# Spectral mixing and a gated feed-forward on one core: the opening's first step by channel halves, the first and last spectrum units in channel parts, three weight blocks converted later

## The chip, the core and the metric

The kernel is one program on one core of a Trainium2 chip. The core has five engines with queues of their own that run side by side: TensorE (PE; its weight loads are shown as PEld), VectorE (DVE), ScalarE (ACT), GpSimd (POOL) and SyncE (SP), which here only issues transfers. Tiles lie in SBUF, matmul results in PSUM (eight banks of 512 float32 values in each of 128 partitions). The metric is the device time of one execution in microseconds, lower is better; it is shown as the median of several runs.

## The reference

Eight elements `x[b]` of 3136 positions by 256 channels are filtered in frequency along the positions, and every position then goes through a feed-forward block with a SoLU gate and a layer norm:

```python
X = np.fft.rfft(x, axis=1)
y = np.fft.irfft(X * (filt_r + 1j * filt_i)[None], n=3136, axis=1)
h = y.reshape(25088, 256) @ w_in                     # 256 -> 1024
e = np.exp(h - h.max(-1, keepdims=True))
solu = h * e / (e.sum(-1, keepdims=True) + 1e-09)
ln = (solu - mean(solu)) / np.sqrt(var(solu) + 1e-06) * g_ln
out = ln @ w_out                                      # 1024 -> 256
```

`w_in` and `w_out` come as float64 and are turned into float32 on the chip.

## The kernel before

All arithmetic is float32. The Fourier transform of 3136 = 49 x 64 positions is done as matmuls with tables in two steps each way. For most elements the data between the steps goes through DRAM. Element 0 stays in SBUF, so that the feed-forward can start early; the part of the program that does this is the opening, and it is all that the change touches.

The opening, in its order:

- **Loads.** SP issues them in order: eight pieces of x (two transfers of 192 KB each), raw weight block 0 behind piece 2 and block 2 behind piece 5 (512 KB each, `begin`, L533), then inverse tables and filters in three groups (L490, L497), weight blocks 1 and 3, small tables, and rows of element 1 (`fetch_second`, L485) into a part of the token array `y` that is not in use yet. At most eight of SP's transfers are under way: an issue waits until the transfer eight places ahead has landed.
- **First step** (L600, L605). Piece i holds 4 of 32 row groups in `rows_x`; two matmuls of 512 columns, each run as two passes, fill the two banks of one PSUM tile, which ScalarE copies back to the same place in SBUF, now named `pairs_x`, in a turned order. The last piece is copied by ScalarE and VectorE, half each. `ps_h` has three such tiles.
- **Filler.** `idle_row` (L614) gives TensorE products that nobody reads; between them `tables_back` (L510, L512) turns the tables for the way back.
- **Transposes** (`turn_rows`, L623): four VectorE transposes of 64 channels each, in place.
- **Spectrum units** (L326 to L365). Seven units, in the order 0, 1, 2, 6, 3, 4, 5. Each has a forward product on TensorE into a two-bank tile (real and imaginary part), four multiplications by the filter on VectorE (L347, L348), two additions on GpSimd (L349; for the last unit the second one on VectorE), an inverse product into two one-bank tiles of `ps_t` (two buffers), and two copies back to `pairs_x` (L365; for the last unit one on VectorE). Two units' forward products run ahead.
- **Way out.** Four more transposes; first step of element 1 (`second.first`, L251, L253), six products and copies with stores to DRAM from GpSimd's queue; then the back products (L419, L423), which fill `y` with tokens.
- **Weights.** `load_float64` (L454 to L464) turns one block of raw words into float32: one step on ScalarE, five on VectorE, two on GpSimd. Blocks 0 and 2 are converted during the first step, 1 and 3 around the last unit. The buffer `power` has two places. Four weight sums (L170) follow, since the feed-forward multiplies 2 x 2 blocks with seven products.

After that the main loop runs, one step per 128 tokens: hidden products (L799), gate and norm on VectorE, ScalarE and GpSimd, projections (L935), with the other elements' transforms put in between at fixed steps (`PLAN`). Instructions of one of these two parts keep their written order on each engine; the main loop's first ones may stand between the opening's last.

Of the kernel before, what the change touches and what calls it, by code (L numbers as in the profile page):

```python
# [9 lines left out]
FP32 = mybir.dt.float32  # L10
# [98 lines left out]
def kernel(  # L109
# [99 lines left out]
    class Spectrum:  # L209
# [114 lines left out]
        def product(self, i, out, lhsT, rhs):  # L324
            for v in range(self.units[i][1]):
                nc.tensor.matmul(out=out[:, v, :], lhsT=lhsT(v), rhs=rhs[:, v, :],  # L326
                                 start=True, stop=True)

        def forward(self, i, pss):
            t2, de = self.t2s.pop(i), self.des[i]  # L330
            for u in range(self.shape(i)[0]):
                for r in range(2):
                    block = slice(NQ * r, NQ * r + NQ)
                    self.product(i, pss[r][NQ * u:NQ * u + NQ], lambda v: de[block, v, 0, u, :],
                                 t2[block, u::2, :] if len(t2.shape) == 3 else t2[block, :, :, u])
            self.spectra[i] = pss

# [16 lines left out]
        def inverse(self, i, pss, out=None, two=False):  # L354
# [9 lines left out]
            for u in range(self.shape(i)[0]):  # L364
                (nc.vector.tensor_copy if two and u else nc.scalar.copy)(  # L365
                    out=self.gs[i][:, u:2 * w:2, :] if out is None else out[:, 0:w, :, u],
                    in_=pss[u][:, 0:w, :])
# [70 lines left out]
    with ExitStack() as st:  # L438
# [8 lines left out]
        def load_float64(dst, raw, power):  # L447
# [4 lines left out]
            ts, stt, tt = (nc.vector.tensor_scalar, nc.vector.scalar_tensor_tensor, nc.gpsimd.tensor_tensor)  # L452
# [109 lines left out]
        for i in range(pieces):  # L562
            for h in range(2):
                fetch_x(h, NCH * i, NCH, nc.sync.dma_start)
            if i in (2, 5):
                begin((0, 2)[i // 3], nc.sync.dma_start)
# [5 lines left out]
        begin(1, nc.sync.dma_start)  # L572
        begin(3, nc.sync.dma_start)
        nc.sync.dma_start(out=wf_t, in_=wf_dram)
        nc.sync.dma_start(out=wi_t, in_=wi_dram)
        nc.sync.dma_start(out=g_sb, in_=moe_g_ln.rearrange("(k p) -> p k", p=P))
        fetch_second(range(EARLY))
# [11 lines left out]

        def conversion(j):  # L590
            power = wpool.tile([P, 512], I32, name="power", tag="power", bufs=2)
            return load_float64(weights[j][0], raws.pop(j), power)

        for j in range(WARM):
            nc.tensor.matmul(out=ps_t.tile([P, P], FP32, name=f"warm_{j}", tag="t"), lhsT=blank, rhs=blank,
                             start=True, stop=True)
        for i in range(pieces):
            ps = ps_h.tile([P, 2, 512], FP32, name=f"pa_0_{i}", tag="h")
            for j in range(2):
                nc.tensor.matmul(out=ps[:, j], lhsT=wf0_t,  # L600
                                 rhs=rows_x[0:NR, NCH * i + 2 * j:NCH * i + 2 * j + 2, :],
                                 start=True, stop=True)
            size = 2 if i < pieces - 1 else 1
            for j in range(0, 2, size):
                (nc.scalar.copy, nc.vector.tensor_copy)[j](  # L605
                    out=pairs_x[:, 2 * i + j:2 * i + j + size].rearrange("p a c t -> p a t c"),
                               in_=ps[:, j:j + size].rearrange("p a (t c) -> p a t c", t=2))
            if i in (3, 6):
                for op in conversion((0, 2)[i // 4]):
                    op()  # L610

        def idle(out):

            nc.tensor.matmul(out=out, lhsT=one, rhs=one, start=True, stop=True)  # L614

        def idle_row(count, name):
            for j in range(count):
                idle(ps_h.tile([P, P], FP32, name=f"{name}_{j}", tag="h"))

        def turn_rows():  # L620
            for first in range(0, C, 64):
                part = pairs_x[:, :, first:first + 64].rearrange("p a c t -> p c a t")
                nc.vector.transpose(out=part, in_=part)  # L623

        for i0, n in ((0, 4), (4, 4)):
            idle_row(12, f"idle_{i0}")
            tables_back(i0, n)
        turn_rows()

        def start(i):  # L630
            i0, n = sp.units[i]
            sp.t2s[i] = pairs_x[:, i0:i0 + n]
            sp.fetch_filter(i)
            sp.fetch_de(i)
            sp.forward(i, halves(f"pb_0_{i}"))

# [3 lines left out]
        for i in order[:2]:  # L640
            start(i)
        tables_back(8, NP - 8)
        early_weights = [op for ops in zip(conversion(1), conversion(3)) for op in ops]
        for at, i in enumerate(order):
            if at + 2 < units:
                start(order[at + 2])
            ended = at == units - 1
            sp.multiply(i, 0, nc.gpsimd.tensor_tensor)
            sp.multiply(i, 1, (nc.vector if ended else nc.gpsimd).tensor_tensor)
            if ended:  # L650
                for op in early_weights[:6]:
                    op()
            pss = [ps_t.tile([P, 2, C], FP32, name=f"pc_0_{i}_{u}", tag="t") for u in range(2)]
            i0, n = sp.units[i]
            sp.inverse(i, pss, pairs_x[:, i0:i0 + n], ended)
        turn_rows()
# [8 lines left out]
        for op in early_weights[6:]:  # L665
            op()
# [567 lines left out]
```

## Time and profile before

| what | us |
|---|---|
| median of the three runs shown | 1574.35 |
| the three runs | 1574.35, 1943.49, 1570.65 |
| profiled execution: its own time | 1569.28 |
| profiled execution: span of the trace | 1567.5 |
| TensorE busy in the span | 1532.5 |
| VectorE, GpSimd, ScalarE busy | 1254.9, 1157.2, 927.9 |

In timeline rows the first number is the start in us from the span's start, the second the duration of the row (of all its instructions where it has a count), then engine, line, operation, tiles, shape and count; the bracket gives the engine's idle time before the row and what ended it. In the table by stretch each engine has its busy time and its number of instructions; the last three columns are TensorE's granted clock, the DMA engines' share and GB/s. A float32 matmul shows as two passes.

### The profile page before, as it was taken

The numbers are of one execution on the slowest core, as the hardware profiler recorded it, in microseconds if no ns is written. First come the engines' busy times: TensorE is split into PE (matmuls) and PEld (weight loads), VectorE is DVE, ScalarE is ACT, GpSimd is POOL, SyncE is SP. The second block draws the span as 40 slices with busy tenths as digits, with TensorE's granted clock in tenths as the row PEclk, the third lists the DMA queues.
The fourth block names the chain that finished last, engine by engine and source line by source line (L and its number), as shares of the span: only waits on it lengthen the run. The fifth ranks groups of instructions, "written<-read, shape, count | busy, mean of one in ns | idle before, by whom it ended". The sixth has DMA issues, their size and how long they took to land.

```text
span 1567.5 us, 36719 instructions
## 1 busy us (share of the span) xinstructions
PE 1532.5 (98%) x12844; PEld 1061.7 (68%) x12844; DVE 1254.9 (80%) x2233; ACT 927.9 (59%) x1898; POOL 1157.2 (74%) x1346
## 2 busy tenths in 40 slices
PE   8988999999999999999999999999999999999997
PEld 5633576667666776667766776667776777777777
DVE  4879878897998789878998698877998777776773
ACT  3565655666556656666566655666556666666663
POOL 2578886697879678887779767786766767676665
PEclk9999999999999999999999999999999999999999
DMA  9768788877987689667886588766874545343434
GB/s 246 252 202 226 218 225 220 227 212 207 252 242 204 173 236 254 196 173 192 249 230 190 152 229 247 203 184 176 233 204 119 138 122 135 88 115 102 116 104 118
DMA packets 342256, 298.07 MB, mean 190 GB/s; under 512 B 27915, under 2 KB 311573, under 8 KB 342073
## 3 DMA queue, kind: packets, MB, share of 16 engines
q1 hardware_dynamic: 278872, 175.82, 42.5%
q0 software_dynamic: 29568, 87.33, 18.6%
q10 hardware_dynamic: 33634, 32.58, 7.2%
q8 instruction: 104, 1.70, 0.5%
q14 instruction: 78, 0.64, 0.1%
HBM read 118.02 MB, written 74.84 MB: 123 GB/s over the span
## 4 chain that ended last, share of the span: by engine, by line
PE 59%; DMA 2%; DVE 0%; SPq 0%; issue 0%; POOL 0%; ACT 0%; ACTq 0%; POOLq 0%
PE o L935 26%; PE m L799 26%; PE py L396 2%; PE pc L326 1%; PE pa L294 1%; PE pb L326 1%; DMA solu_t<-turn 1%; DMA x<-in_x_dram 0%; SPq L880 0%; DMA out_dram<-ot 0%; PE o L899 0%; POOL u L778 0%; ACT e L833 0%; DVE h L845 0%; DVE h L820 0%
## 5 line engine op out<-in xcount | busy, mean ns | idle before, releaser
L935 PEld LDWEIGHTS o<-w_out_sb,solu_t 128*128 128x128 f32 x3136 | 381.1, 192 | 47.3 <-issue 43.5
L799 PE MATMUL m<-w_in_sb,s 128*128 128x512 f32 x784 | 398.4, 609 | 5.8 <-ACT h L809 3.3
L935 PE MATMUL o<-w_out_sb,solu_t 128*128 128x128 f32 x3136 | 400.2, 276 | 1.7 <-DVE ot L955 1.6
L935 PEld LDWEIGHTS o<-w_out_sb,u 128*128 128x128 f32 x2352 | 306.4, 191 | 138.3 <-issue 108.6
L799 PE MATMUL m<-w_in_sb,y 128*128 128x512 f32 x588 | 307.8, 607 | 5.6 <-DVE nmax L823 3.8
L935 PE MATMUL o<-w_out_sb,u 128*128 128x128 f32 x2352 | 309.6, 275 | 2.6 <-POOL u L778 1.8
L845 DVE SCALAR_TENSOR_TENSOR h<-e,h 128x1024 f32<-128x1024 f32 x196 | 308.7, 1575 | 0.4 <-ACT e L833 0.4
L951 ACT ACTIVATE ot<-o,rs_t 128x128 f32<-128x128 f32 x392 | 143.6, 367 | 248.2 <-PE o L935 246.1
L809 ACT COPY h<-m 128x512 f32<-128x512 f32 x294 | 173.2, 589 | 195.6 <-PE m L799 191.0
L778 POOL TENSOR_TENSOR u<-solu_t 128x512 f32<-128x512 f32 x98 | 135.0, 1377 | 184.7 <-DMA solu_t<-turn 126.2
L823 DVE CUSTOM_DVE_ANT_0 h<-m,h 128x512 f32<-128x512 f32 x196 | 134.3, 685 | 165.4 <-ACT h L809 103.1
L853 ACT ACTIVATE h<-h,nmu 128x1024 f32<-128x1024 f32 x196 | 225.1, 1148 | 53.4 <-DVE turn L863 53.4
L863 DVE STREAM_TRANSPOSE turn<-h 128x1024 f32<-128x1024 f32 x196 | 243.0, 1240 | 3.8 <-DVE ot L955 0.3
L833 ACT ACTIVATE e<-h,nmax 128x1024 f32<-128x1024 f32 x196 | 225.3, 1149 | 8.1 <-DVE h L845 6.6
L778 POOL TENSOR_TENSOR u<-solu_t,u 128x512 f32<-128x512 f32 x98 | 136.0, 1388 | 94.0 <-PE o L935 93.4
L799 PEld LDWEIGHTS m<-w_in_sb,s 128*128 128x128 f32 x784 | 127.9, 191 | 90.9 <-issue 71.6
L955 DVE SCALAR_TENSOR_TENSOR ot<-o,rs_t,ot 128x128 f32<-128x128 f32 x299 | 103.7, 347 | 97.0 <-ACT ot L951 59.8
L778 POOL TENSOR_TENSOR u<-u,solu_t 128x512 f32<-128x512 f32 x98 | 161.9, 1652 | 15.9 <-PE o L935 9.0
L799 PEld LDWEIGHTS m<-w_in_sb,y 128*128 128x128 f32 x588 | 96.7, 191 | 102.1 <-issue 46.2
L778 POOL TENSOR_TENSOR solu_t<-solu_t,solu_t 128x512 f32<-128x512 f32 x98 | 155.0, 1581 | 0.9
L778 POOL TENSOR_TENSOR s<-y 128x128 f32<-128x128 f32 x196 | 100.2, 511 | 6.1 <-DMA x<-in_x_dram 5.7
L396 PEld LDWEIGHTS py<-wb_t,t 50*64 50x64 f32 x3584 | 57.6, 135 | 42.9 <-issue 18.7
(121 smaller groups left out, 1953.9 us busy)
## 6 DMA issues: line engine op xcount, KB each, us to landing
solu_t<-turn SPq DMA_DIRECT2D x780, 128.0 KB
out_dram<-ot SPq DMA_DIRECT2D x196, 128.0 KB
t<-d POOLq DMA_DIRECT2D x112, 200.0 KB, 6.8
d<-x POOLq DMA_DIRECT2D x100, 200.0 KB, 5.3
t<-d ACTq DMA_DIRECT2D x37, 512.0 KB
f<-f_dram POOLq DMA_DIRECT2D x37, 512.0 KB, 7.6
d<-g POOLq DMA_DIRECT2D x36, 512.0 KB, 5.0
x<-in_x_dram SPq DMA_DIRECT2D x112, 98.0 KB
```

Source lines behind the costliest of these rows:

```text
L396: nc.tensor.matmul(out=views[g][64 * h:64 * h + 64, cb, i, :], lhsT=t4[rows, i, c0:c0 + 64], rhs=wb_t[rows, 0:N1], start=True, stop=True)
L778: nc.gpsimd.tensor_tensor(out=out, in0=in0, in1=in1, op=op)
L799: nc.tensor.matmul(out=ms[j, bank], lhsT=lhsT, rhs=w_in_sb[:, w, :], start=m in (1, 2, 7), stop=True, skip_group_check=True)
L809: nc.scalar.copy(out=h_half(k, i), in_=ms[j, 0])
L823: nc.vector.tensor_tensor_reduce(out=h_half(k, i), in0=ms[j, bank], in1=h_half(*kept), scale=1.0, scalar=sofar, op0=ALU.add, op1=ALU.min, ...
L833: nc.scalar.activation(out=e, in_=hs[k], func=AFT.Exp, bias=nmaxs.pop(k)[:, 1:2], scale=-1.0, accum_out=esums[g][:, i:i + 1])
L845: nc.vector.scalar_tensor_tensor(out=solu, in0=e, scalar=SHRINK, in1=solu, op0=ALU.mult, op1=ALU.mult, accum_out=nmu)
L853: nc.scalar.activation(out=solu, in_=solu, func=AFT.Square, bias=nmu, scale=-float(DFF), accum_out=variances[g][:, i:i + 1])
L863: nc.vector.transpose(out=turns[g][:, :, i, :], in_=solus[k].rearrange("p (f j) -> p f j", j=32))
L935: nc.tensor.matmul(out=pos[p, bank], lhsT=lhs[:, f, :], rhs=w[:, f, :], start=f == 0 and (m in (1, 2, 7) or alone), stop=True, skip_group_ ...
L951: nc.scalar.activation(out=out_half(p, *to)[0], in_=pos[p, 0], func=AFT.Copy, scale=rs)
L955: nc.vector.scalar_tensor_tensor(out=ot, in0=pos[p, bank], scalar=rs, in1=out_half(p, *kept)[0], op0=ALU.mult, op1=ALU.add)
```

## The change

1. Raw block 2 is loaded behind the filters, ahead of blocks 1 and 3.
2. The first step goes by channel halves: each piece has a matmul and a ScalarE copy for channels 0 to 127 and then for 128 to 255. The first halves go to a free part of the token array `y` (`first_half`), the second halves to `pairs_x`. For the last two pieces both first halves come before both second halves. VectorE copies none of them.
3. The first two transposes read `first_half` and write `pairs_x`; the last two stay in place. The fetch of element 1's rows, part of which goes to the same place in `y`, is written behind the first two.
4. The filler rows are 12, 6 and 6 products in place of 12 and 12, and use the two buffers of `ps_t`, as the turned tables do. The third row stands between two parts of the first two units' forward products: channels 0 to 191, then 192 to 255.
5. The last unit goes by channel halves through products, inverse and copies; both copies are ScalarE's.
6. Block 2 is converted last, with VectorE in GpSimd's place; of blocks 1 and 3, the two ScalarE steps come after the third and second last unit, and the ten VectorE steps behind the last transposes.

```diff
-        def forward(self, i, pss):
-            t2, de = self.t2s.pop(i), self.des[i]
+        def forward(self, i, pss, cs=slice(0, C)):
+            t2, de = self.t2s[i], self.des[i]
...
+        def multiply_half(self, i, cs, adds):
+            rows, f, spectra = slice(0, P), self.fs[i], self.spectra[i]
+            if i not in self.prods:
+                self.prods[i] = [self.buffer(i, kind, [P, 2, C]) for kind in ("pr", "pi")]
+                self.terms = [self.buffer(i, "pt", [P, 2, C]) for _ in range(2)]
+            re, im = (ps[rows, :, cs] for ps in spectra)
+            for part, (out, term, add) in enumerate(zip(self.prods[i], self.terms, adds)):
+                out, term = out[rows, :, cs], term[rows, :, cs]
+                nc.vector.tensor_tensor(out=out, in0=re, in1=f[rows, :, part, cs], op=ALU.mult)
+                nc.vector.tensor_tensor(out=term, in0=im, in1=f[rows, :, 1 - part, cs], op=ALU.mult)
+                add(out=out, in0=out, in1=term, op=(ALU.subtract, ALU.add)[part])
+
+        def inverse_half(self, i, pss, cs, out, copies):
+            de, prods = self.des[i], self.prods[i]
+            for r in range(2):
+                for u in range(2):
+                    rows = slice(NQ * u, NQ * u + NQ)
+                    self.product(i, pss[u][NQ * r:NQ * r + NQ], lambda v: de[rows, v, 1, r, :],
+                                 prods[r][rows], cs)
+            for u, copy in enumerate(copies):
+                copy(out=out[:, :, cs, u], in_=pss[u][:, :, cs])
...
-            if i in (2, 5):
-                begin((0, 2)[i // 3], nc.sync.dma_start)
+            if i == 2:
+                begin(0, nc.sync.dma_start)
...
-        begin(1, nc.sync.dma_start)
-        begin(3, nc.sync.dma_start)
+        for j in (2, 1, 3):
+            begin(j, nc.sync.dma_start)
...
+        first_half = y[:, 1, 0:NH * P].rearrange("p (a c t) -> p a c t", c=P, t=2)
+        places = [first_half, pairs_x[:, :, P:C, :]]
+        for i, h in [(i, h) for i in range(pieces - 2) for h in range(2)] + [
+                (i, h) for h in range(2) for i in range(pieces - 2, pieces)]:
+            if i not in pas:
+                pas[i] = ps_h.tile([P, 2, 512], FP32, name=f"pa_0_{i}", tag="h")
+            nc.tensor.matmul(out=pas[i][:, h], lhsT=wf0_t,
+                             rhs=rows_x[0:NR, NCH * i:NCH * i + NCH, P * h:P * h + P],
+                             start=True, stop=True)
+            nc.scalar.copy(out=places[h][:, 2 * i:2 * i + 2].rearrange("p a c t -> p a t c"),
+                           in_=pas[i][:, h].rearrange("p (a t c) -> p a t c", t=2, c=P))
+            if (i, h) == (3, 1):
+                for op in conversion(0):
+                    op()
...
-                idle(ps_h.tile([P, P], FP32, name=f"{name}_{j}", tag="h"))
+                idle(ps_t.tile([P, P], FP32, name=f"{name}_{j}", tag="t"))
...
+        turn_rows(range(2), first_half)
         fetch_second(range(EARLY))
...
+        turn_rows(range(2, 4))
+        idle_row(12, "idle_0")
+        tables_back(0, 4)
+        idle_row(6, "idle_1")
+        tables_back(4, 4)
+        ahead_of_last = slice(0, 192), slice(192, C)
...
+        for cs in ahead_of_last:
+            for i in order[:2]:
+                sp.forward(i, pbs[i], cs)
+            if cs.stop < C:
+                idle_row(6, "idle_2")
...
+                if at >= units - 3:
+                    weight_ops[at + 3 - units]()
+            else:
+                for n, cs in enumerate((slice(0, P), slice(P, C))):
+                    sp.multiply_half(i, cs, (nc.gpsimd.tensor_tensor, nc.vector.tensor_tensor))
+                    sp.inverse_half(i, pss, cs, pairs_x[:, i0:i0 + 2], [nc.scalar.copy] * 2)
+        turn_rows(range(4))
+        for op in weight_ops[2:12]:
+            op()
...
-        for op in early_weights[6:]:
+        for op in weight_ops[12:] + conversion(2, nc.vector.tensor_tensor):
             op()
```

## The prediction

> **What bounds the kernel.** I read the page's busy shares first, then a table of busy time by stretch, then the timeline by engine up to 76 us. The table of stretches (busy us per engine, granted clock, DMA share, GB/s):
>
> ```profile
> 0.00:7.60 7.60, 4.63 (x20) 4.36 (x21) 0.18 (x3) 1.47 (x2) 2.03 (x7) 1.00 0.79 165
> 7.60:24.50 16.90, 15.73 (x45) 7.48 (x45) 6.56 (x12) 9.37 (x10) 3.95 (x4) 1.00 1.08 269
> 24.50:35.60 11.10, 8.08 (x73) 7.36 (x76) 8.89 (x4) 1.17 (x2) 1.28 (x1) 0.91 0.95 266
> 35.60:55.00 19.40, 16.54 (x195) 11.55 (x188) 19.02 (x35) 8.61 (x16) 15.05 (x13) 0.96 0.66 196
> 55.00:75.50 20.50, 20.50 (x141) 16.75 (x142) 16.69 (x23) 11.44 (x23) 8.49 (x10) 1.00 0.92 317
> 75.50:160.00 84.50, 73.43 (x352) 33.24 (x351) 69.48 (x131) 47.94 (x99) 63.31 (x79) 0.96 0.71 211
> 160.00:1567.50 1407.50, 1393.62 (x12029) 980.98 (x12027) 1134.04 (x2029) 847.90 (x1747) 1063.09 (x1233) 1.00 0.68 186
> ```
>
> From 160 us on, TensorE is busy 1393.6 of 1407.5 us: a microsecond won or lost ahead of it moves the end by about that much, and the change can win nothing there. Everything it touches lies before 76 us. A time 2% away (31 us, about what a measurement of this kernel can tell from no change) would need the opening to become 40% longer or shorter. The opening's chain, from the timeline:
>
> ```profile
> 7.61 10.63 PE L600 MATMUL pa<-x,wf_t 98*128 98x512 f32 x24 [1.92 <-DMA x<-in_x_dram]
> 19.40 3.67 PE L600 MATMUL pa<-x,wf_t 98*128 98x512 f32 x8 [1.15 <-ACT x L605]
> ...
> 23.11 0.63 ACT L605 COPY x<-pa 128x512 f32<-128x512 f32 x1
> 23.77 0.69 DVE L605 COPY x<-pa 128x512 f32<-128x512 f32 x1 [2.55 <-DMA f<-in_filt_i_dram]
> 24.50 8.89 DVE L623 STREAM_TRANSPOSE x<-x 128x2048 f32<-128x2048 f32 x4
> ...
> 33.53 3.66 PE L326 MATMUL pb<-x,de 64*64 64x256 f32 x32 [3.02 <-DVE x L623]
> 35.62 0.69 DVE L347 TENSOR_TENSOR pr<-pb,f 128x512 f32<-128x512 f32 x1 [2.23 <-PE pb L326]
> ...
> 54.98 5.52 PE L251 MATMUL pa<-y,wf_t 98*100 98x512 f32 x12 [0.71 <-ACT x L365]
> ```
>
> First products on TensorE (7.61 to 23.07), copies, four transposes (24.50 to 33.39), forward products, then from 35.62 the multiplications on VectorE with their additions on GpSimd (36.99 to 52.03 without a gap), the last inverse products and copies, and at 54.98 TensorE goes over to the second element and stays full until 75.5.
>
> **The loads.** Weight block 2 (512 KB) lands at 17.60, after x piece 5 (15.86) and before pieces 6 and 7 (19.26, 20.76): 1.74 us. Behind the filters, it lets the two pieces land at 17.52 and 19.02. SP's later issues keep their order and bytes. The fetch into the token array that must now wait for the first two transposes is issued at 36.8 in before, later than any end of those transposes below, so it does not hold SP up.
>
> **The first step by halves.** Before: a piece is four passes of 0.43 us, 1.72 us; eight make 13.8 us plus 1.3 us of waiting for piece 6 (ready about 18.1, starts 19.40). The copy starts 2.00 us after the piece does (7.61 to 9.61). After: two passes, a copy of 512 elements (0.63, the row at 23.11), two passes, another copy. What decides is whether the second half's product may run while ScalarE copies the first half out of the same two-bank tile. Two rows say no. The VectorE copy above reads the other bank of the tile and writes other addresses than ScalarE's, TensorE was done at 23.07, and yet it starts at 23.77, 0.03 after ScalarE's end. And the first multiplication (35.62) reads the real bank alone, but starts after the last of the passes that fill the imaginary one. I take it that the program orders all accesses to one such tile. Then a piece costs: product to copy 1.14 (2.00 less 0.86; the same from 54.98 to the copy at 56.12), copy 0.63, copy to product 0.09 (56.71 to 56.80), second product 0.86: 2.72 us in place of 1.72. The ScalarE step of weight conversion 0 (0.66) falls into the copies and adds 0.45. Piece 6 starts at 7.61 + 6 x 2.72 + 0.45 = 24.4 (18.1 without that wait). The last two pieces go first half, first half, second half, second half: the first halves are copied out by 27.05, the last product ends at 27.96, the last copy at 28.87.
>
> The Trainium skill ("PSUM — Partial Sum Buffer", section "PSUM bank collisions raise a hardware error") states that two engines on different banks run clean; by it the halves need no such wait, and rival A is the outcome. The two rows show the program waiting all the same.
>
> **Transposes and forward products.** The first two transposes need the first halves alone and run from 27.05; four take 8.89 and end at 35.95 (before 33.39). On TensorE behind the last product stand, in order: 24 idle passes (0.112 each, 2.7), one table turn (0.9), a wait of 0.9 for its copy, because the idle tiles now share its two buffers, ten idle passes (1.1), a turn (0.9): 34.4. The third transpose is done at 33.7. Forward products of 192 channels: eight groups of four passes, 0.22 each at 256 columns with a busy TensorE (38.72 to 38.94), 0.43 after the 3.0 us of idling that before has; I take 0.2, so 36.0. Twelve idle passes: 37.4. The last 64 channels of unit 0: four groups, between 0.055 (by columns) and 0.22 (as now, if loading weights sets it), I take 0.15, plus 0.25 to the reader: multiplication starts at 38.25, bounds 37.9 to 38.6. Against 35.62: **+2.6 us** (2.3 to 3.0). The early forward gains little, as the idle passes behind it outlast the fourth transpose.
>
> **The last unit in halves**, on before's clock. Its products are ready about when they were: GpSimd gets to them at 50.77 either way, and 0.72 per half (64x256 row) makes 51.5 and 52.2 against 52.03. TensorE starts at 52.74, held by the copies of the unit before (51.97 to 53.11), as now. The first half's two copies (0.40, the 128x256 row) run at about 54.0 to 54.75; the second half's products write the same two tiles and wait for them, about 54.5 to 55.7; copies 55.55 to 56.3; TensorE gets the tile for the second element at 56.0 in place of 54.98: **+1.0 us**. Bounds: 0 (if the halves overlapped entirely) to 1.6 (products at their present 1.5 us). The four transposes start no later than before, since the first two need the first half alone.
>
> **Three weights later.** VectorE gets ten conversion steps behind the transposes in place of six (+1.5 us), GpSimd's four additions end about 72.7 (71.5), then conversion 2 on VectorE: 2.4 for five steps and 1.3 for two tensor operations, held until 68.9 by the power buffer: about 73; sums by 76. ScalarE's step (0.66) hides beside the back products, where it idles 0.46 in each 0.94. Needed: block 2 by 77.3 (second product, 75.47 + 0.86, + 1.0), the first sum by 80.9. Cost 0; if the cover goes, rival B.
>
> **Sum.** +2.6 + 1.0 = +3.6 us on the profiled execution's 1569.28 (span 1567.5): 1572.9. Of the three runs shown, the lowest (1570.65) and the median (1574.35) lie 1.4 and 5.1 us above it; with some 2 us for that the time is **1575 us**.
>
> **Rivals.** A, no wait between halves: products run through to 21.7, transposes 20.9 to 29.8, the TensorE row behind ends at 31.2, multiplication starts at 32.0, -3.6 + 1.0 = -2.6: 1566.7 by the profiled run, 1569 measured. For it: separate banks. Against: the two rows. Chance 0.14. B, the late weights become the bound, slower than before and than the forecast: one VectorE conversion step beside GpSimd took 1.39 in place of 0.43 (18.18). If all five do, and tensor operations take 0.99 (the row of three weight sums, 2.97), conversion 2 ends at 77.9, the sums at 81.8, and the w_out conversion behind them on VectorE at 84.7. GpSimd's part of it (79.54, shifted to 80.5) then starts 4.2 late, and it is busy 20.6 of the 24 us from 76 to 100, with the second element's stores in its queue. It decides from the point where conversion 2 takes over 8.4 us. +7.8: 1577.1, measured 1579. Against: 81.8 needs every step contended. Chance 0.14. The skill ("SBUF — State Buffer", section "Who interferes with whom") lets a VectorE operation with two SBUF inputs and GpSimd's reads exclude each other; that agrees with 0.99 against 0.68, and by it alone B gets only part of its price. C, the change does not do what it says: the first transposes wait for all copies (28.87) and gain no lead, +1.0 more: 1576. Chance 0.08.
>
> **Chances.** Forecast 0.60, A 0.14, B 0.14, C 0.08; 0.04 for something beyond 2% that no row shows. Range 1565 to 1584: A less 4 for the spread of runs, B plus 5. Faster by over 2% 0.01, within 2% 0.96, slower 0.03.
>
> **What would show it.** Right: each second-half product starts just after a ScalarE copy, pieces 2.7 us apart, transposes from about 27, multiplication from about 38.3, the second element's first product about 58.6. Wrong: products without gaps and transposes from 21 (A), the first hidden product or the second element's forward products waiting for VectorE or GpSimd (B), transposes from 29 (C).

## The result, and the profile after

The changed kernel takes 1589.67 us (median; 1584.35 to 1594.36) against 1573.47 for the kernel before: a ratio of 1.0104, 95% interval 1.0078 to 1.013. One of the six runs of the kernel before is the slow one of 1943.49 us; it is in that median and not in the ratio. The changed kernel is 1% slower, 16 us at the medians: less than the 2% named in the prediction, but outside its range of 1565 to 1584. The interval is about 4 us to either side, so a difference well below the 31 us that the prediction took for the limit can be told here.

The profiled execution took 1591.07 us (span 1589.3) against 1569.28 (span 1567.5). First the table of busy time by stretch of the changed kernel, cut at its own turning points (start and end of the stretch, its length, busy us of PE, PEld, DVE, ACT and POOL, granted clock of TensorE, DMA share, GB/s):

```profile
7.60:24.50 16.90, 13.89 (x16) 4.60 (x17) 2.40 (x5) 4.28 (x7) 0.00 (x0) 0.56 1.10 264
24.50:35.60 11.10, 9.69 (x12) 3.08 (x11) 0.00 (x0) 3.63 (x6) 2.56 (x2) 0.50 1.10 300
35.60:50.20 14.60, 14.48 (x134) 11.15 (x133) 8.89 (x4) 3.68 (x6) 0.00 (x0) 0.95 0.52 156
50.20:70.30 20.10, 16.43 (x209) 11.40 (x198) 19.12 (x36) 9.04 (x19) 15.23 (x14) 1.00 0.87 288
70.30:90.80 20.50, 20.46 (x140) 16.72 (x141) 19.02 (x23) 12.15 (x25) 8.89 (x10) 1.00 0.26 85
```

The column to read is the granted clock: 0.56 and 0.50 in the first step, where before had 1.00 and 0.91 in the same stretches. In the first two stretches, 28 us, TensorE has 27 instructions, all passes of the first step (one stands in both rows); before it had 116 in the same time, 32 of them those passes. The page's slices tell the same in one digit (before, the row was nines throughout):

```profile
PEclk6999999999999999999999999999999999999999
```

The timeline of the same opening (start, duration, engine, line, operation, tiles, shapes, count; in brackets the idle time ahead of it and what ended it):

```profile
7.82 1.10 PE L616 MATMUL pa<-x,wf_t 98*128 98x512 f32 x2 [2.12 <-DMA x<-in_x_dram]
8.95 0.61 ACT L619 COPY y<-pa 128x512 f32<-128x512 f32 x1 [4.78 <-PE pa L616]
9.61 3.72 PE L616 MATMUL pa<-x,wf_t 98*128 98x512 f32 x4 [0.70 <-ACT y L619]
14.03 3.78 PE L616 MATMUL pa<-x,wf_t 98*128 98x512 f32 x4 [0.70 <-ACT y L619]
...
31.97 7.17 PE L616 MATMUL pa<-x,wf_t 98*128 98x512 f32 x10 [0.70 <-ACT y L619]
...
37.99 4.51 DVE L636 STREAM_TRANSPOSE x<-y 128x2048 f32<-128x2048 f32 x2 [24.31 <-DMA g_sb<-in_moe_g_ln_dram]
...
38.97 3.34 PE L627 MATMUL idle<-one 128*128 128x128 f32 x24
...
42.42 4.46 DVE L636 STREAM_TRANSPOSE x<-x 128x2048 f32<-128x2048 f32 x2
...
46.32 1.67 PE L326 MATMUL pb<-x,de 64*64 64x192 f32 x32
...
47.91 1.80 PE L627 MATMUL idle<-one 128*128 128x128 f32 x12
49.65 0.77 PE L326 MATMUL pb<-x,de 64*64 64x64 f32 x32
50.23 0.69 DVE L349 TENSOR_TENSOR pr<-pb,f 128x512 f32<-128x512 f32 x1 [3.35 <-PE pb L326]
...
70.34 5.52 PE L251 MATMUL pa<-y,wf_t 98*100 98x512 f32 x12 [0.48 <-ACT x L377]
```

Every group of products starts right behind a copy of ScalarE, as forecast: the wait between the two halves of a piece is there. But pieces stand 4.48 us apart (14.03 less 9.61 is 4.42; the four distances up to 31.97 are 4.48 to 4.50), not 2.72, because a pass takes 0.86 us instead of 0.43. The transposes start at 37.99 instead of 27.05, the first multiplication at 50.23 instead of 38.25.

What follows keeps this lag and adds little. Against before the first multiplication is 14.6 us late (50.23, 35.62), the second element's first product 15.4 (70.34, 54.98), the first hidden product 15.35 (90.82, 75.47), the eleventh hidden product 16.15 (102.94, 86.79). (A hidden product's number is that of its pass in the rows.) The rest of the 21.8 us between the two profiled executions builds up slowly over the following 1400 us, and the medians have only 16.2.

### The profile page after: what moved, and what is told of

Its sections match the earlier page's. It is cut to its first block, busy times and chain, and to the rows that moved or that the text cites. A ratio compares the mean times of both kernels' runs of the same rounds, so it can differ in the third digit from the quotient of the medians.

```text
span 1589.3 us, 36833 instructions
## 1 busy us (share of the span) xinstructions
PE 1548.4 (97%) x12892; PEld 1066.4 (67%) x12892; DVE 1261.3 (79%) x2238; ACT 928.9 (58%) x1909; POOL 1153.8 (73%) x1345
## 4 chain that ended last, share of the span: by engine, by line
PE 45%; DMA 2%; DVE 1%; SPq 1%; issue 1%; POOL 0%; ACT 0%; ACTq 0%; DVEq 0%; POOLq 0%
PE o L972 21%; PE m L836 20%; PE py L421 2%; DMA solu_t<-turn 1%; PE pc L326 1%; PE pb L326 1%; PE pa L294 1%; DMA x<-in_x_dram 1%; SPq L917 0%; DMA out_dram<-ot 0%; POOL u L815 0%; DVE turn L900 0%; PE o L936 0%; DVE h L860 0%; SPq L270 0%
## 5 line engine op out<-in xcount | busy, mean ns | idle before, releaser
L815 POOL TENSOR_TENSOR solu_t<-solu_t,solu_t 128x512 f32<-128x512 f32 x98 | 150.2, 1532 | 0.9
```

The lines of the kernel that those rows point to most:

```text
L815: nc.gpsimd.tensor_tensor(out=out, in0=in0, in1=in1, op=op)
```

## The experiments

Three questions had to be kept apart: whether the wait between the halves is the cause, what took the clock down, and what the other parts cost. The ratios are to the kernel before on the same chip, where its median was between 1571.1 and 1571.7 us.

### Taking the wait away: own_tiles, pairs

own_tiles gives each half a tile of one bank, and each of the two spectra too:

```diff
-        ps_h = pool("ps_h", 3, PSUM, stack=st)
+        ps_h = pool("ps_h", 6, PSUM, stack=st)
...
-            if i not in pas:
-                pas[i] = ps_h.tile([P, 2, 512], FP32, name=f"pa_0_{i}", tag="h")
-            nc.tensor.matmul(out=pas[i][:, h], lhsT=wf0_t,
+            pas[i, h] = ps_h.tile([P, 512], FP32, name=f"pa_0_{i}_{h}", tag="h")
+            nc.tensor.matmul(out=pas[i, h], lhsT=wf0_t,
```

> The changed kernel, but each half of the first step gets a one-bank PSUM tile of its own instead of one half of a two-bank tile; the same products and copies in the same order. Theory 1, the wait between the halves and the half clock that it brings are the whole of the loss in the opening: the products run without gaps, a piece takes 1.7 us in place of 4.5, the granted clock stays at 0.95 or more up to 35 us, the transposes start at 21 to 22 us in place of 38.0, the first multiplication at 32 to 33 in place of 50.2, and the time is 1567 to 1572 us, 17 to 22 below the changed kernel. Theory 2, the clock falls for a reason that has nothing to do with the wait (the order of the loads, the narrow products): the clock again falls to 0.64, a piece takes 3.5 us or more, and the time is 1582 or more. Theory 3, the loss comes from the late weights or the last unit: the opening gains, but the time stays within 4 us of the changed kernel's 1590.

pairs keeps the tiles and changes the order of the products:

```diff
-        for i, h in [(i, h) for i in range(pieces - 2) for h in range(2)] + [
-                (i, h) for h in range(2) for i in range(pieces - 2, pieces)]:
+        for i, h in [(i, h) for two in range(0, pieces, 2) for h in range(2) for i in (two, two + 1)]:
```

> The changed kernel with its two-bank tiles, but the products of two pieces are taken in the order first half, first half, second half, second half, for all pieces and not only for the last two, so that the copy that a second half waits for runs beside the product of another piece. Theory 1 (the wait and its half clock): a pair of pieces takes about 3.6 us in place of 9.0, the clock stays at 0.95 or more up to 35 us, transposes from 22 to 23 us, first multiplication at 33 to 34, time 1568 to 1574 us. Theory 2 (the clock falls for another reason): a pair takes 7 us or more, clock about 0.64, time 1582 or more. Theory 3 (late weights, last unit): time within 4 us of 1590 although the opening gains.

own_tiles took 1574.48 us, a ratio of 1.0025 (1.001 to 1.004); pairs 1575.56, 1.0028 (1.0012 to 1.0043). Either edit takes away 12 to 13 of the 16 us. Three rows of the timeline of own_tiles, the first products, the first transposes and the first multiplication:

```profile
7.67 15.67 PE L615 MATMUL pa<-x,wf_t 98*128 98x512 f32 x32 [2.02 <-DMA x<-in_x_dram]
...
22.31 4.51 DVE L635 STREAM_TRANSPOSE x<-y 128x2048 f32<-128x2048 f32 x2 [8.53 <-DMA f<-in_filt_i_dram]
...
34.41 0.69 DVE L349 TENSOR_TENSOR pr<-pb,f 128x512 f32<-128x512 f32 x1 [3.20 <-PE pb L326]
```

All 32 passes stand in one row without a gap, while ScalarE copies from the other banks. So nothing in the hardware makes a product into one bank wait for a copy out of another; the two-bank tile did, as one object to which the program orders every access. The Trainium skill ("PSUM — Partial Sum Buffer", section "PSUM bank collisions raise a hardware error") says that two engines on different banks run clean, and this run agrees: passes 0.43 us apart beside copies of 0.62. In pairs, too, all 32 passes stand in one row (8.12 to 25.31); its transposes start at 24.16 and the first multiplication at 36.42, later than the 22 to 23 and 33 to 34 expected.

Theory 1 stands, and theory 2 falls, but theory 1's time of 1567 to 1572 was too low. Two things show in the rows. The passes still began with one stretch at half clock, of which more below. And the first multiplication comes at 34.41, only 1.2 us ahead of before, although the fourth transpose is done at 31.21: the TensorE row behind the first step ends later than the transposes.

### Leaving the wait and giving TensorE work: filler, warm16

filler leaves the wait and puts four products that nothing reads into each of the first six:

```diff
+            if h and i < pieces - 2:
+                for j in range(4):
+                    nc.tensor.matmul(out=ps_t.tile([P, P], FP32, name=f"fill_{i}_{j}", tag="t"), lhsT=blank,
+                                     rhs=blank, start=True, stop=True)
```

> The changed kernel with the wait left in place: behind the first-half product of pieces 0 to 5 stand four products of a blank tile (128x128, nothing reads them), about 0.9 us at full clock, so that TensorE has work while ScalarE copies. They add work and take nothing away. Theory 1a, the wait alone costs 1.0 us a piece and the rest of the loss is the half clock: the clock stays at 0.95 or more up to 35 us, a piece takes 2.7 to 2.9 us, piece 6 starts at 24 to 26, transposes from 27 to 29, first multiplication at 38 to 40, time 1576 to 1580 us. Theory 1b, the wait by itself costs the whole 15 us and the clock only goes with it: pieces stay above 4 us and the time is 1588 or more. Theory 2 (the clock falls for another reason than idle time of TensorE): clock about 0.64, pieces above 4.5 us, time 1590 or more.

warm16 leaves the first step alone altogether and lengthens the warm-up ahead of it:

```diff
-WARM = 10
+WARM = 16
```

> The changed kernel with 16 warm-up products in place of 10, so that TensorE hardly idles between them (their end is at 5.5 us now) and the first product at 7.6; tiles, order and waits as changed. The question is what takes the clock down and holds it there. Theory 1a, the idle stretch ahead of the first product together with the first waits takes the clock down, and waits of 1.0 us in every 2.7 would not do it alone: the clock stays full, pieces take 2.7 us, the first multiplication starts at 38 to 40 us, time 1576 to 1580. Theory 1c, the waits alone do it: pieces of 4.4 to 4.5 us, granted clock about 0.64 up to 35 us, first multiplication at 49 or later, time 1586 to 1593.

filler took 1580.65 us, 1.0056 (1.0038 to 1.0075): more work in less time than the changed kernel. Its pieces stand 2.71 us apart and the transposes start at 28.89, as theory 1a has it, though the first multiplication, at 41.13, is 1.1 us later than its 38 to 40; 1b and 2, with pieces above 4 us, fall. warm16 took 1578.74, 1.0042 (1.0024 to 1.006), 11 us less than the changed kernel for six more products that nothing reads. The timeline of warm16:

```profile
8.09 1.10 PE L616 MATMUL pa<-x,wf_t 98*128 98x512 f32 x2 [0.45 <-DMA x<-in_x_dram]
9.89 1.98 PE L616 MATMUL pa<-x,wf_t 98*128 98x512 f32 x4 [0.70 <-ACT y L619]
12.58 1.98 PE L616 MATMUL pa<-x,wf_t 98*128 98x512 f32 x4 [0.71 <-ACT y L619]
15.27 1.98 PE L616 MATMUL pa<-x,wf_t 98*128 98x512 f32 x4 [0.70 <-ACT y L619]
...
27.03 4.51 DVE L636 STREAM_TRANSPOSE x<-y 128x2048 f32<-128x2048 f32 x2 [13.31 <-DMA f<-in_filt_i_dram]
...
39.28 0.69 DVE L349 TENSOR_TENSOR pr<-pb,f 128x512 f32<-128x512 f32 x1 [3.35 <-PE pb L326]
```

The waits are the same 0.70 us, but the four passes take 1.98 instead of 3.78, pieces stand 2.69 apart and the transposes start at 27.03. Those are the numbers of the prediction (2.72 and 27.05). The difference between the two kernels at the transposes, 10.96 us, is the half clock alone. The medians differ by 10.9 as they stand, and by 8.9 when each is taken against before on its own chip.

Theory 1a is confirmed and 1c falls: waits of this size do not pull a warm TensorE down. The table of busy time, cut at the 3.41 us steps in which the clock changes in the records, shows what did. First the changed kernel:

```profile
6.30:9.71 3.41, 1.19 (x3) 0.40 (x3) 0.00 (x0) 0.61 (x1) 0.00 (x0) 1.00 1.05 275
9.71:13.13 3.42, 3.42 (x4) 1.02 (x4) 1.89 (x4) 0.62 (x1) 0.00 (x0) 0.50 1.08 242
13.13:16.54 3.41, 2.71 (x4) 1.17 (x4) 0.51 (x2) 1.01 (x2) 0.00 (x0) 0.50 1.09 250
16.54:19.95 3.41, 2.71 (x4) 0.84 (x3) 0.00 (x0) 0.83 (x2) 0.00 (x0) 0.50 1.11 252
```

and warm16 in the same place:

```profile
6.46:9.88 3.42, 2.28 (x11) 1.26 (x10) 0.00 (x0) 0.61 (x1) 0.00 (x0) 1.00 1.05 276
9.88:13.29 3.41, 2.69 (x6) 1.15 (x7) 1.97 (x4) 1.25 (x2) 0.00 (x0) 1.00 1.09 221
13.29:16.70 3.41, 2.71 (x7) 0.89 (x6) 0.43 (x1) 1.49 (x3) 0.00 (x0) 1.00 1.09 236
```

In the changed kernel the window from 6.30 holds the idle stretch before the first product and the first wait; TensorE is busy for 1.19 of 3.41 us, and the next window runs at half clock. The first trace of before has a window at nearly the same place (6.24 to 9.65), behind an idle stretch of 1.92 us in place of 2.12; its passes follow without a wait, TensorE is busy for 2.04 us, and the clock stays full. From then on the changed kernel is busy for 2.71 us or more of each window and stays at half. In warm16 TensorE is busy for the same 2.71 us and stays at full clock. The busy time is the same, but not the work: at full clock four passes take 2.69 us with their wait, which makes 5.1 passes in 3.41 us; at half clock the passes take twice as long, the wait as long as ever, and four in 4.48 us make 3.0. So half clock, once there, keeps the number of passes in a window low, and the last section shows that the windows of the first step sort by that number. In filler, with the gaps filled, the one window at half clock (9.18 to 12.60) was the last of the opening.

### The rest of the change: whole_first, own_last_whole, own_early2

whole_first has the first step, the idle rows, the transposes and the first forward products as before, and leaves the late weights and the last unit in halves:

```diff
-            nc.tensor.matmul(out=pas[i][:, h], lhsT=wf0_t,
-                             rhs=rows_x[0:NR, NCH * i:NCH * i + NCH, P * h:P * h + P],
-                             start=True, stop=True)
...
+            for j in range(2):
+                nc.tensor.matmul(out=ps[:, j], lhsT=wf0_t,
+                                 rhs=rows_x[0:NR, NCH * i + 2 * j:NCH * i + 2 * j + 2, :],
+                                 start=True, stop=True)
...
-        turn_rows(range(2), first_half)
...
+        idle_row(12, "idle_4")
+        tables_back(4, 4)
+        turn_rows(range(4))
...
+        for i in order[:2]:
+            sp.forward(i, start(i))
```

> The changed kernel with the first step, the idle rows, the transposes and the first forward products as they were before; weight block 2 behind the filters, the later conversions and the last unit in halves are kept. Theory 1 (the first step's wait and half clock): the first multiplication at 34 to 36 us, and the time within 3 us of the kernel before, of which the last unit in halves makes +0.8 and the earlier pieces 6 and 7 up to -1.3. Theory 3, a good part of the loss is in the late weights and the last unit: the time is 6 us or more above the kernel before.

It took 1577.55 us, 1.004 (1.0024 to 1.0056): 6.4 us above before at the medians (interval 3.8 to 8.8). That is over the 3 us of theory 1 and meets the 6 us of theory 3, but its trace doesn't bear that size out. The first multiplication is at 37.30, 1.7 late, because the first passes ran at half clock up to about 14 us (their weight loads stand 0.85 apart from 8.61 to 13.73, and 0.43 from 14.31). To the second element's first product it loses another 0.76 (57.42 less 37.30 is 20.12, before 19.36), at the hidden products 0.78. So these parts cost 1.5 us in the trace, and the start of the clock as much again; the rest of the 6.4 has no row of its own and stays open.

own_last_whole takes own_tiles and makes the last unit whole again:

```diff
-                for n, cs in enumerate((slice(0, P), slice(P, C))):
-                    sp.multiply_half(i, cs, (nc.gpsimd.tensor_tensor, nc.vector.tensor_tensor))
-                    sp.inverse_half(i, pss, cs, pairs_x[:, i0:i0 + 2], [nc.scalar.copy] * 2)
+            ended = at == units - 1
+            sp.multiply(i, 0, nc.gpsimd.tensor_tensor)
+            sp.multiply(i, 1, (nc.vector if ended else nc.gpsimd).tensor_tensor)
+            sp.inverse(i, pss, pairs_x[:, i0:i0 + n], ended)
```

> One-bank tiles for the halves of the first step, and the last spectrum unit whole again, with its copies on ScalarE and VectorE, as before the change. If the last unit in halves costs what the trace of the changed kernel says (+0.75 us), the stretch from the first multiplication to the second element's first product is 19.4 us, as before, in place of 20.1, and the time is about 0.7 below that of the one-bank tiles alone: 1573 to 1575 us by the kernel before's median on this chip at about 1571. If the halves cost nothing, 20.1 us and no difference.

The stretch did become 19.33 us (34.70 to 54.03) in place of 20.11, so the halves cost 0.78. The time did not follow: 1578.15, 1.0044 (1.0029 to 1.0059), which is 3.4 us more than own_tiles, each against before on its own chip, where 0.7 less was expected. The gain is given back some 27 us later, at the second pair of hidden products, which now waits 1.76 us instead of 0.57: the 0.78 and 0.4 more. The two intervals overlap, and the rest of the 3.4 has no row. The same wait in own_tiles, on TensorE, and VectorE's work ahead of it:

```profile
67.29 1.52 DVE L480 TENSOR_SCALAR power<-raw 128x512 int32<-128x512 int32 x1 [1.20 <-POOL raw L488]
68.85 1.40 DVE L482 TENSOR_SCALAR power<-power 128x512 f32<-128x512 f32 x1
70.28 1.40 DVE L483 TENSOR_SCALAR power<-power 128x512 int32<-128x512 int32 x1
...
79.74 0.48 DVE L487 TENSOR_SCALAR power<-w_out_sb 128x256 int32<-128x256 int32 x2
80.15 0.68 DVE L859 CUSTOM_DVE_ANT_0 h<-m,h 128x512 f32<-128x512 f32 x1
```

```profile
80.98 1.10 PE L835 MATMUL m<-w_in_sb,s 128*128 128x512 f32 x2 [0.57 <-POOL raw_out L488]
```

Three of the five steps of weight conversion 2 take 1.4 to 1.5 us beside GpSimd's additions instead of 0.43. They and the two additions that VectorE now does push the w_out conversion behind them on VectorE, and that pushes the normalizing step of the first hidden tile (L859) from 77.53 in before to 80.15. It ends at 80.83, and the product that waits starts at 80.98. The row names GpSimd as releaser, whose operation (80.11 to 80.84) ended beside it.

own_early2 takes own_tiles and puts block 2 back to its place behind piece 5, with its conversion in the first step and its additions on GpSimd:

```diff
-            if i == 2:
-                begin(0, nc.sync.dma_start)
+            if i in (2, 5):
+                begin((0, 2)[i // 3], nc.sync.dma_start)
...
-            if (i, h) == (3, 1):
-                for op in conversion(0):
+            if (i, h) in ((3, 1), (6, 0)):
+                for op in conversion((0, 2)[i // 4]):
                     op()
...
-        for op in weight_ops[12:] + conversion(2, nc.vector.tensor_tensor):
+        for op in weight_ops[12:]:
```

> One-bank tiles for the halves of the first step, and weight block 2 loaded behind piece 5 of x and converted in the first step, with its additions on GpSimd, as before the change. Theory 3a, the late conversion on VectorE costs 0.8 us at the hidden products: no product waits there at 80 to 82 us, and the distance from the first to the eleventh hidden product is 11.3 us, as before, in place of 12.1. Against it stands a later arrival of pieces 6 and 7 of x, at most 1.0 us in the opening. Time 1573 to 1576. Theory 3b, the 0.8 us comes from something else, such as the last unit in halves: 12.1 us stay.

The wait is gone. VectorE's normalizing step starts at 77.21, and the product that waited in own_tiles starts at 80.39, before the first of GpSimd's two operations ends (79.74 to 80.49). So it was VectorE's step that it waited for. TensorE's row at the second hidden pair in own_early2:

```profile
79.53 1.88 PE L835 MATMUL m<-w_in_sb,s 128*128 128x512 f32 x4
```

From the first to the eleventh hidden product it takes 11.32 us, as before, where own_tiles and the changed kernel have 12.1. Theory 3a holds, and pieces 6 and 7 cost nothing here, since the window at half clock made TensorE later than their loads. The time is 1574.22, 1.0015 (0.9999 to 1.0032).

### A second trace of the kernel before: before_again

> The kernel before, unchanged, for a second trace of it. If the 1 to 5 us by which the traces of the experiments fall behind the first trace of before from 114 us on are differences from run to run, this trace falls behind the first one in the same way, by 1 to 3 us, with half-clock windows of TensorE at other places. If they are an effect of the edits, it stays within 0.5 us of the first trace from 114 us to the end.

1572.71 us. The time is ordinary, but the opening is not that of the first trace. Its table of busy time, cut at the clock's windows, and its first products:

```profile
4.45:7.86 3.41, 0.81 (x6) 0.62 (x5) 0.00 (x0) 0.00 (x0) 0.00 (x0) 1.00 1.05 196
7.86:11.28 3.42, 3.21 (x4) 1.51 (x5) 0.03 (x1) 0.00 (x0) 0.00 (x0) 0.50 1.05 284
11.28:14.69 3.41, 3.41 (x5) 1.35 (x4) 2.37 (x5) 1.09 (x1) 0.00 (x0) 0.50 1.09 269
14.69:18.10 3.41, 3.41 (x9) 1.52 (x8) 0.61 (x2) 2.17 (x2) 0.00 (x0) 1.00 1.06 288
```

```profile
8.06 17.26 PE L600 MATMUL pa<-x,wf_t 98*128 98x512 f32 x32 [2.81 <-DMA x<-in_x_dram]
```

The unchanged kernel also falls to half clock at its first products, for two windows. But its passes follow without a gap, and the clock comes back. It reaches the first multiplication at 37.87 instead of 35.62, and the first hidden product 2.25 us behind the first trace. Later it is 1.2 behind at 114 us, 3.9 at 1188 and 3.4 at the end. So differences of 2 to 4 us between single traces arise without any edit. At the first multiplication only the lags of the changed kernel (14.6 us), filler (5.5) and warm16 (3.7) are larger than this trace's 2.25.

### A version that keeps the early transposes: tight, tight_again, tight_early2

tight puts together one-bank tiles, the whole last unit and 16 warm-up products, and shortens TensorE's row:

```diff
-        idle_row(12, "idle_0")
-        tables_back(0, 4)
-        idle_row(6, "idle_1")
-        tables_back(4, 4)
+        idle_row(9, "idle_0")
+        tables_back(0, 4)
+        tables_back(4, 4)
+        idle_row(6, "idle_1")
...
-            if cs.stop < C:
-                idle_row(6, "idle_2")
```

> One-bank tiles, last unit whole, 16 warm-up products, and a shorter row on TensorE behind the first step: 18 idle passes, both table turns, 12 idle passes, the forward products of 192 channels, and the last 64 channels with no idle passes between. If the waits found so far are all that keeps the early transposes from paying, transposes start at about 21 us, the first multiplication at 30.5 to 31.5 (35.6 before), the second element's first product at 50 to 51 (55.0 before), and the time is 3 to 5 us below the kernel before. If something behind the opening bounds instead (loads, weights, GpSimd), the gain is under 2 us although the multiplications start early.

> The kernel with one-bank tiles, whole last unit, 16 warm-up products, the shorter row and the late conversion of weight block 2 once more, for a closer comparison with the early conversion and with the kernel before on one chip: 0 to 3 us below the kernel before, the second pair of hidden products 1.5 to 2 us late.

tight_early2 adds the early conversion of block 2, as in own_early2.

> The kernel with one-bank tiles, whole last unit, 16 warm-up products and the shorter row, and weight block 2 loaded behind piece 5 and converted in the first step, as before the change. Theory 3a, the late conversion on VectorE holds up the hidden products: the wait of 1.7 us ahead of the second pair of hidden products is gone or below 0.6, pieces 6 and 7 arrive late and cost 0.5 to 1.3 us in the opening, the eleventh hidden product starts 3 to 4 us ahead of the kernel before (2.6 without this edit), time 2 to 4 us below the kernel before. Theory 3c, behind the opening the loads of the second element and GpSimd set the pace whatever the opening does: the eleventh hidden product no earlier than 2.6 us ahead, time within 1 us of the kernel with the late conversion.

tight took 1569.33 us, 0.9993 (0.9979 to 1.0007), tight_again 1570.92, 0.9992 (0.9977 to 1.0007), tight_early2 1572.03, 0.9999 (0.9986 to 1.0011). None can be told from the kernel before, and the 3 to 5 us expected of tight and the 2 to 4 of tight_early2 did not come. The timeline of tight:

```profile
21.49 4.51 DVE L635 STREAM_TRANSPOSE x<-y 128x2048 f32<-128x2048 f32 x2 [7.74 <-DMA f<-in_filt_r_dram]
...
30.99 0.69 DVE L349 TENSOR_TENSOR pr<-pb,f 128x512 f32<-128x512 f32 x1 [0.61 <-PE pb L326]
```

```profile
74.44 2.09 POOL L808 TENSOR_TENSOR s<-y 128x128 f32<-128x128 f32 x1 [5.91 <-ACT y L253]
```

```profile
77.12 1.98 PE L829 MATMUL m<-w_in_sb,s 128*128 128x512 f32 x4 [1.71 <-POOL s L808]
```

The opening does what the early transposes are for: the first multiplication at 30.99, 4.6 us ahead of the first trace of before, and the first hidden product 4.7 ahead. Of that, 1.9 us go at the second hidden pair, which needs GpSimd's sums of tokens: the first of them takes 2.09 us instead of 0.45, while VectorE converts weights beside it. In tight_early2 the wait there is gone and the eleventh hidden product comes 3.1 ahead (tight 2.6, tight_again 2.3), but pieces 6 and 7 arrive later, and the transposes start 0.9 to 1.2 us behind those of the other two (22.68; 21.82 and 21.49), of which up to 0.4 is its later first product: theory 3a is right in the rows, and the time shows no gain. What is left of the lead is gone by 1188 us: from 114 us to there the three kernels lose 4.2 to 5.4 against the first trace of before, and the second trace of before loses 2.7. Why this long, nearly full stretch gives the lead back is open; no single row carries it.

## Why the prediction was wrong

**The wait was right, its price was not.** The step that failed is the sum of a piece in the part on the first step by halves: 1.14 to the copy, 0.63, 0.09, and a second product of 0.86, 2.72 us in all. Its two products are priced at 0.43 a pass, from rows in which TensorE never stood still. The measured piece is 4.48, with passes of 0.86. In the table of stretches that the prediction itself shows, the granted clock was a column, 0.91 where TensorE idled; and it used the fact once, for the forward products behind 3 us of idling. It did not ask what the new idle time would do to the clock, and the list of rivals has no such case. The size of the term is the 10.96 us from 27.03 in warm16 to 37.99: the five distances up to the last group of products take 22.36 us (9.61 to 31.97) instead of 13.61 (9.89 to 23.50), 8.75 more, and from there to the transposes it is 6.02 instead of 3.53, 2.49 more; the start of the first group, 0.28 earlier, goes off.

**At full clock the steps were near.** In warm16 the transposes run from 27.03 to 35.93 (forecast 27.05 and 35.95). That it agrees so closely is in part luck: the first product starts 0.5 us late, and the five distances between pieces are 13.61 us instead of 14.05, mostly because ScalarE's conversion step adds 0.18 (20.82 less 17.95 is 2.87) and not 0.45. The multiplication starts at 39.28, forecast 38.25: the fourth transpose was indeed outlasted by TensorE's row, but by 3.35 us instead of 2.3. The 24 idle passes take 3.18 us (28.02 to 31.20), not 2.7, and the rest of the row adds about as much. The first products came 0.2 (the changed kernel) and 0.5 us (warm16) later than in the first trace of before.

**Last unit in halves.** Forecast +1.0 (0 to 1.6), measured +0.75 in the changed kernel (70.34 less 50.23 is 20.11, before 19.36) and 0.78 by its undoing.

**Three weights later.** Forecast 0, measured 0.8, and 1.2 more when the stretch ahead is shorter (own_last_whole). It begins as rival B does, at a tenth of its price: three steps of five were slowed, not all, and the tensor operations took 0.69. But the delay reaches TensorE through VectorE's own queue and not, as B has it, through GpSimd's. The failing assertion is "cost 0": VectorE's normalizing step of the first hidden tile stands behind the conversions in the same queue, and the working looked at the weights alone.

**The sum.** Forecast +3.6 us. At full clock, by warm16's trace, the eleventh hidden product is 5.2 late: 3.66 to the multiplication, 0.74 for the last unit, 0.8 for the weights; at the medians it is 7.3 (interval 3.8 to 9.4). The half clock adds 11 in the traces, and 8.9 at the medians when each is taken against before on its own chip. Of the 14.7 us by which 1575 was too low, those 8.9 are the missing term and 3.7 (7.3 less 3.6) what else the terms lacked, of which the trace shows 1.6. The other 2.1 are the kernel before itself: its median is 1573.47, and the prediction started from 1571.4 (1575 less 3.6).

**The rivals.** A, no wait, is what own_tiles makes: its copies and transposes come as described, 1.4 us later for the window at half clock, but its multiplication at 34.41 instead of 32.0, because TensorE's row behind the first step is longer than it says, and its time 1574.48 instead of 1569. C did not occur: the transposes start with the first halves' last copy (37.34 to 37.96), with two copies still to come.

The range's upper end was built from rival B and the spread of runs. The mechanism that decided costs 11 us in the trace, more than rival B's 7.8.

## What to carry to other kernels

A wait of 0.7 us in a chain of products is not priced by its own length alone: ask whether TensorE, with that gap in every few microseconds, will still be granted its full clock, and whether it was warm when the stretch began. If a buffer of two PSUM banks serves two engines in turn, give each bank a tile of its own, or let another product come between; both took the wait away here. And when an operation is pushed back on an engine, look at what stands behind it in that engine's queue, not only at who needs its result.

## What the runs showed of the hardware that was not expected

The granted clock follows what TensorE did in the window before. At full clock, windows of 3.41 us with TensorE busy for 2.04 (the first trace of before, from 6.24), 2.28, 2.69 or 2.71 us were followed by full clock; windows with 1.19 (the changed kernel), 1.39 (own_tiles, from 5.48), 0.97 (filler) or 0.81 us (before_again) were followed by half. So the bound lies between 41% and 60% here.

At half clock the busy time does not sort them. Windows with 2.71 us were followed by half, and so were two that are busy throughout by their rows (the changed kernel's from 9.71 and 23.37, 3.42 and 3.40) and one with 3.21 (before_again, from 7.86). Windows with 2.69 (whole_first, from 34.50) and 2.79 us (before_again, from 35.17), in the forward products, were followed by full.

For the first step the number of passes sorts them better. Take the windows in which TensorE has passes of the first step and nothing else. Those in which only three of them start were followed by half clock (the changed kernel's from 6.30 and from 13.13, for example), those with five or more by full. With four, seven were followed by full (the changed kernel's from 33.61 and own_tiles' from 8.89 among them) and one by half, before_again's from 7.86, whose first pass starts 0.2 us into it. This holds at either clock, so the records don't show that the clock remembers anything beyond one window. It is a sorting of these traces and not a tested rule; the ends of products are modelled in the trace, and other shapes are not counted.

The Trainium skill ("TensorE: Matmul & The Clock Gate", section "Part 1: The HAM clock gate (the "warmup" mystery)") says that the clock halves after an idle window of about 3.4 us, returns after a busy one, and that the window of 3413 ns runs freely, whatever the kernel does. The records agree with the length and the free running: the windows start at 6.30, 6.46, 5.48 and 4.45 in four of the traces. They differ on the first point. No window that took the clock down in the first step was idle; they were busy for 24 to 41%. The same page (section "HAM oscillation — how this bites in real kernels") names idle gaps of over about 3.4 us as the ones to avoid; here gaps of 0.70 us by the rows were enough to keep the clock down, and idle stretches of 2.0 to 2.8 us, with what lay around them, to take it down. The measurement decides for this kernel.

A kernel's opening is not the same in every run: the same program, the kernel before, had its first passes at full clock in one trace and at half for 6.8 us in another, 2.25 us apart at the first multiplication. In the second the windows stand elsewhere (from 4.45 and 7.86, not 6.24) and the first product comes 0.45 us later; which of the two decided is open. In two traces (pairs, whole_first) the clock's records begin only at 13.49 and 14.02 us, and the column shows full clock for passes that stand 0.85 apart. The distance of the passes is the surer reading there.
